# Hashed attention and SwiGLU on one Trainium2 core: key signs of the early pairs moved from VectorE to ScalarE, query signs spread by a transfer

## The chip, the cores and the metric

The kernel runs on one core of one Trainium2 chip. The metric is the device time of one execution in microseconds (us); smaller is better. The times are those of whole executions without the profiler; the profile is one further execution, recorded by the hardware profiler, whose span is a little different from the timed median.

## What is computed

Two blocks follow each other. The first is attention in which a key counts for a query only if both fall in the same hash bucket; the second is a SwiGLU feed-forward block on its output.

```python
q_bits = (einsum('bhsd,dk->bhsk', q, proj) > 0)      # 6 bits; k_bits likewise
mask   = q_bucket[..., :, None] == k_bucket[..., None, :]
scores = where(mask, (q @ k.T) / sqrt(64), -1e9)
attn   = exp(scores - max) ; attn /= sum(attn) + 1e-9
x      = (attn @ v)   # (4, 8, 768, 64) -> (3072, 512)
out    = (silu(x @ w_gate) * (x @ w_val)) @ w_out     # d_ff 1536
```

There are 4 batches of 8 heads, 768 positions and head size 64; everything is float32 (the weights come as 64-bit floats and are narrowed on the chip).

## The kernel before

**Units of work.** Two heads make a *pair* (`n` = 0 to 15, four to a batch), because two heads of size 64 fill 128 partitions. A pair is worked in two *halves* of 384 queries, and each half in six *chunks* `c` of 128 keys. For each chunk `score` (L461) makes a score tile for either head on TensorE: first the product of the transposed float32 queries and keys (`qT`, `kT`), then a second bf16 matmul into the same PSUM tile with the *sign tiles* `qb`, `kb`. ScalarE takes the exponential (L464) into the weight tile `A` (or its early place, called `room`). VectorE adds the weight tiles of the six chunks (`add`, L489 and L493) into `acc`. After the six chunks come six chunks of `attend` (L475): weights times values into one PSUM bank `av`, which ScalarE copies out (L482).

**The mask by signs.** `hash_w` projects the 64 numbers of a head to 6; either head has a group of 16 rows in a block of 32. `Sign` on ScalarE (L397) turns the projected queries and keys into +1 and -1 in rows 0 to 31 of `qb`, `kb`. A seventh row of the group is a constant. VectorE then spreads these rows to where the matmul of either head reads them (rows 0 to 63 for head 0, rows 64 to 127 for head 1): the keys' rows are multiplied, once for head 0 and once for head 1, by a column that is OFF/2 = 2^34 for this head's bits, -6 times that for its constant row and 0 for the other head (L406, two instructions), and the queries' rows are copied (L409, one instruction). The second matmul so adds 0 where all six bits agree and -2^35 or less where they don't.

**Sum and normalisation.** For pair n-1, `total` is issued in the first half of pair n, behind the second chunk's scores: a matmul with ones sums `acc` over the partitions (L506, into the `av` bank, for batch 0), VectorE takes the reciprocal (L514), eight transfers on the SyncE queue spread it over the partitions (L519), and `norm` on VectorE multiplies (L526). In batch 0 the `av` bank is free for the next `attend` only when the reciprocal has read it.

**Order of the work.** The order is written out by hand, and each engine works through its own list in order. In the first batch (pairs 0 to 3), there is no feed-forward work yet for TensorE; VectorE and ScalarE fill up with narrowing the weights (L279, L280, L293, L295, L298, L327). From pair 4 on, TensorE's list is filled up with the feed-forward matmuls of the batch before (L550). The next pair's operands are made one pair ahead (`front(n + 1)`): for pairs 1 to 4 by TensorE transposes (L378) that ScalarE copies out (L381), and by `hash_at_once`, which projects (L391) and takes the four signs behind the last chunk of the second half; its spread waits in the list `rest` until the end of that half, so that VectorE reaches it behind the six `add`s. For pairs 5 to 15, `hash_blocks` hands signs and spread to the feed-forward stretch one by one, and the queries' signs are spread by a SyncE transfer (L411). PSUM has seven rotating banks and the `av` bank. `load(n + 2)` puts the loads of queries, keys and values on the SyncE queue behind the second half's `attend`.

Two lines of the main loop say where the preparation is issued:

```python
if u + c == 2 or not gating and half == 1 and c == NCH - 1:
    prepare_pair(1)
```

Of the kernel before, what the change touches and what calls it, by code (L numbers as in the profile page):

```python
# [8 lines left out]
FP32 = mybir.dt.float32  # L9
# [3 lines left out]
ALU = mybir.AluOpType  # L13
AF = mybir.ActivationFunctionType
AX = mybir.AxisListType
# [3 lines left out]
def kernel(  # L19
# [31 lines left out]
    OFF = 2.0**35  # L51
    SCALE = 1.0 / D**0.5
# [4 lines left out]
    konst = ctx.enter_context(tc.tile_pool(name="konst", bufs=1))  # L57
# [12 lines left out]
    def bank(name):  # L70
        return banks.tile([P, 512], FP32, tag="ps", name=name)
# [50 lines left out]
    ident = konst.tile([P, P], FP32, tag="ident", name="ident")  # L122
# [9 lines left out]
    for _ in range(9):  # L132
        ps = bank("idle")
# [4 lines left out]


    HR = 16  # L140
    assert NBITS + 1 <= HR and 2 * HR == BLOCK
    rules = wraw.tile([P, PIECE, 2], I32, tag="words", name="rules").rearrange("p f w -> p (f w)")
    rules = rules.bitcast(FP32)[:, 0 : 3 * P].rearrange("p (x r) -> p x r", r=P)

    nc.gpsimd.memset(rules[:, 0, :], -(2.0**-120))
    nc.gpsimd.memset(rules[:, 1:3, :], 0.0)
    groups = rules.rearrange("p x (g r) -> p x g r", r=HR)
    nc.gpsimd.memset(groups[:, 0, :, NBITS : NBITS + 1], 1.0)
    for h in range(2):
        g = groups[:, 1 + h, h, :]  # L150
        nc.gpsimd.memset(g[:, 0:NBITS], OFF / 2)
        nc.gpsimd.memset(g[:, NBITS : NBITS + 1], -NBITS * OFF / 2)
    nc.vector.tensor_tensor(rules, rules, ident.unsqueeze(1).to_broadcast([P, 3, P]), op=ALU.mult)
    columns = konst.tile([P, 3], FP32, tag="columns", name="columns")
    nc.vector.tensor_reduce(out=columns, in_=rules, axis=AX.X, op=ALU.add)
    nudge, *times_k = (columns[0:BLOCK, x : x + 1] for x in range(3))

    hash_w = konst.tile([P, BLOCK], FP32, tag="hash", name="hash")
    nc.vector.memset(hash_w, 0.0)
# [14 lines left out]
    for t in (sides["k", 0], sides["q", 0], sides["q", 1]):  # L174
# [19 lines left out]
                      name="room")  # L194
# [160 lines left out]
    def prepare_on(n):  # L355
        for _ in range(n):
            next(preparing, None)
# [7 lines left out]
    T = {}  # L365
    bits = {}
# [3 lines left out]
    def front(n):  # L370


        def transpose(name, half):
            if (name, n) not in T:
                T[name, n] = opnd.tile([P, S], FP32, tag=name + "T", name=name + "T")
            ps = bank("tps")
            for i in range(CH):
                nc.tensor.transpose(ps[:, i * P : (i + 1) * P],  # L378
                                    raws[name, n][:, half * CH + i, :, :].rearrange("p h d -> p (h d)"),
                                    ident)  # L380
            nc.scalar.copy(T[name, n][:, half * HQ : (half + 1) * HQ], ps[:, 0:HQ])  # L381

        bits["q", n] = sides["q", n % 2]
        bits["k", n] = sides["k", n % 2]

        def hash_blocks(todo, own):


            tile_ = bank("hps")
            for i, (name, half) in enumerate(todo):  # L390
                nc.tensor.matmul(tile_[i * BLOCK : (i + 1) * BLOCK, 0:HQ], hash_w,  # L391
                                 T[name, n][:, half * HQ : (half + 1) * HQ],
                                 start=True, stop=True)
            low, high = slice(0, BLOCK), slice(D, D + BLOCK)

            def sign(i, name, half):
                nc.scalar.activation(bits[name, n][low, half * HQ : (half + 1) * HQ],  # L397
                                     tile_[i * BLOCK : (i + 1) * BLOCK, 0:HQ], AF.Sign, bias=nudge)

            def spread():  # L400
                for name in sorted({name for name, _ in todo}):
                    hs = [half for x, half in todo if x == name]
                    b = bits[name, n][:, hs[0] * HQ : (hs[-1] + 1) * HQ]
                    if name == "k":
                        for to, times in ((high, times_k[1]), (low, times_k[0])):
                            nc.vector.tensor_scalar(b[to], b[low], scalar1=times, scalar2=None,  # L406
                                                    op0=ALU.mult)
                    elif own:
                        nc.vector.tensor_copy(b[high], b[low])  # L409
                    else:  # L410
                        nc.sync.dma_start(b[high], b[low])  # L411

            return [lambda i=i, at=at: sign(i, *at) for i, at in enumerate(todo)] + [spread]

        def hash_at_once(todo):
            *signs, spread = hash_blocks(todo, True)
            for f in signs:
                f()
            return [spread]

        def transpose_blocks(name):
            T[name, n] = opnd.tile([P, S], FP32, tag=name + "T", name=name + "T")
            nc.vector.transpose(T[name, n], raws[name, n].rearrange("p c h d -> p (c h d)"))

        order = [("q", 0), ("q", 1), ("k", 0), ("k", 1)]
        if n > NP:

            return ([lambda name=name: transpose_blocks(name) for name in "qk"]
                    + [lambda: hash_blocks(order, False)])
        turns = [lambda x=x: transpose(*x) for x in order]  # L430
        if n == 0:
            return [turns[2], turns[0], lambda: hash_at_once([("k", 0)]),
                    lambda: hash_at_once([("q", 0)]), turns[3], turns[1],
                    lambda: hash_at_once([("k", 1), ("q", 1)])]
        return turns[2:] + turns[:2] + [lambda: hash_at_once(order)]


    units = [(n, half, c) for n in range(len(pairs)) for half in range(2) for c in range(NCH)]
# [9 lines left out]
    def weights(u):  # L448
        return ((early_ring if u < MOVE else late_ring) + ring)[u % NCH]

    def score(u):
        n, half, c = units[u]
        qs = slice(half * HQ, (half + 1) * HQ)
        ks = slice(c * P, (c + 1) * P)
        sc = [bank("sc")[:, 0:HQ] for _ in range(2)]
        for x, start in ((T, True), (bits, False)):
            if u < 2 and not start:
                prepare_pair(1)
            for h in range(2):
                rows = slice(h * D, (h + 1) * D)  # L460
                nc.tensor.matmul(sc[h], x["k", n][rows, ks], x["q", n][rows, qs],  # L461
                                 start=start, stop=not start)
        for h in range(2):
            nc.scalar.activation(weights(u)[:, h, 0:HQ], sc[h], AF.Exp, scale=SCALE)  # L464

    def attend(u):
        n, half, c = units[u]
# [16 lines left out]
    def add(u):  # L484
        n, half, c = units[u]
        a = weights(u)
        if c == 1:
            acc[n, half] = att.tile([P, 2, HQ], FP32, tag="acc", name="acc")
            nc.vector.scalar_tensor_tensor(out=acc[n, half], in0=weights(u - 1)[:, :, 0:HQ],  # L489
                                           scalar=S * EPS / P, in1=a[:, :, 0:HQ],  # L490
                                           op0=ALU.add, op1=ALU.add)
        elif c > 1:
            nc.vector.tensor_tensor(acc[n, half], acc[n, half], a[:, :, 0:HQ], op=ALU.add)  # L493
# [241 lines left out]
    for u in range(0, N, NCH):  # L735
        n, half, _ = units[u]
        gating = u >= LATE
# [3 lines left out]
                nc.gpsimd.memset(t[:, :, HQ:AW], 1.0)  # L741
        for c in range(NCH):
            score(u + c)
            if u + c == 2 or not gating and half == 1 and c == NCH - 1:
                prepare_pair(1)
                if u == 0:
                    finish(rest)
            if c == 1 and half == 0 and 0 < n <= NP:
                total(n - 1)
            if c:  # L750
                add(u + c)
        if n <= NP:
            finish(waiting)
        if not gating and half == 0:
            steps = front(n + 1)
        if not gating and half == 0 and u > 0:
# [9 lines left out]
        if not gating and half == 0:  # L766
            prepare_pair(2 if u > 0 else 4)
        finish(first)
        finish(rest)
        prepare_on(0 if u == LATE else 4)  # L770
        chores = []
        if half == 1 and n >= NP:
# [67 lines left out]
```

The softmax here doesn't subtract the row's maximum and nothing guards it: scores larger than these inputs give would overflow.

## Time and profile before

| what | before |
|---|---|
| time, median of 3 (lowest to highest) | 1007.15 us (1006.15 to 1009.98) |
| span of the profiled execution | 1005.8 us |
| TensorE busy in 0 to 120, 120 to 920, 920 to the end | 109.52 of 120, 799.4 of 800, 82.5 of 86 us |
| VectorE busy in 30:40, 50:60, 80:90, 100:110 | 9.53, 9.35, 9.57, 9.35 of 10 us |
| ScalarE busy in the same stretches | 9.29, 6.53, 6.86, 5.89 of 10 us |
| share of the 16 DMA engines in them | 0.64, 0.77, 0.98, 1.00 |

How to read it: a line of a timeline gives the start, the time from the first start to the last end of a run of like instructions, the engine, the line of the kernel, the operation with `out<-in`, and in square brackets how long the engine sat idle before it and what ended that wait. In the table of groups, the number after "x" is the count, then busy us and the mean ns of one, then the idle time before. In the list of waits, the columns are total us, number of times and longest. The chain of waits goes back from the last instruction to whatever released each step, so it shows which engine held the others up in which stretch. TensorE's matmul ends are modelled, and its "busy" includes matmuls that run longer at a lower granted clock.

### The profile page before, as it was taken

To read this page: it belongs to the slowest core of one execution; us is meant where nothing else is said; L and a number is where in the kernel's file an instruction comes from. 1 tells how busy PE (TensorE), PEld (TensorE's weight loads), DVE (VectorE), ACT (ScalarE), POOL (GpSimd) and SP (SyncE) were. 2 spreads that over 40 slices of the span, in tenths; PEclk is the share of its full clock that TensorE was granted. 3 is DMA by queue.
4 is the path that set the end of the run, shared out by engine and by line. 5 is a ranking of instruction groups with operands and counts; after the bars stand their busy time and mean duration, and the time that the engine had idled before them with its cause. 6 is when DMAs were issued, how large, how long until landed. Compare 5 with 4: busy or idle time off the path is not lost.

```text
span 1005.8 us, 12454 instructions
## 1 busy us (share of the span) xinstructions
PE 991.4 (99%) x4597; PEld 600.8 (60%) x4597; DVE 577.2 (57%) x904; ACT 392.3 (39%) x877; POOL 101.0 (10%) x195
## 2 busy tenths in 40 slices
PE   9988899999999999999999999999999999999998
PEld 4444455555566775555557776555555787555687
DVE  5888898888884615556454543545556442435431
ACT  6877456555433214334341223334443211222200
POOL 3222132231000000000000000000000000111000
PEclk9999999999999999999999999999999999999999
DMA  7776586876313032423430304242122011323001
GB/s 228 215 243 215 157 214 186 230 241 180 103 37 84 24 76 83 105 91 90 105 107 23 75 20 116 76 104 83 56 85 80 22 37 63 104 77 115 29 28 36
DMA packets 120557, 106.75 MB, mean 106 GB/s; under 512 B 89200, under 2 KB 103888, under 8 KB 120496
## 3 DMA queue, kind: packets, MB, share of 16 engines
q0 software_dynamic: 19104, 73.28, 22.8%
q1 hardware_dynamic: 100592, 32.48, 14.1%
q8 instruction: 36, 0.59, 0.2%
q10 hardware_dynamic: 800, 0.20, 0.1%
q14 instruction: 25, 0.20, 0.1%
HBM read 81.79 MB, written 17.30 MB: 99 GB/s over the span
## 4 chain that ended last, share of the span: by engine, by line
PE 89%; DVE 6%; DMA 1%; SPq 1%; issue 1%; ACT 1%; DVEq 0%; POOL 0%
PE up L550 43%; PE po L550 21%; PE sc L461 12%; PE av L475 10%; DVE acc L493 1%; SPq L519 1%; PE sum L506 1%; PE hps L391 1%; DMA words<-in_moe_w_out_dram 1%; DVE wo L514 1%; DVE room L295 1%; DVE room L327 1%; DMA wo<-wo 1%; DVE room L293 0%; PE idle L134 0%
## 5 line engine op out<-in xcount | busy, mean ns | idle before, releaser
L550 PE MATMUL up<-xT,room 128*128 128x384 f32 x768 | 260.9, 488 | 0.0
L550 PEld LDWEIGHTS up<-xT,room 128*128 128x128 f32 x768 | 144.6, 190 | 106.7 <-issue 9.8
L550 PE MATMUL up<-xc,room 128*128 128x384 f32 x576 | 197.4, 486 | 0.0
L461 PE MATMUL sc<-qT,kT 64*128 64x384 f32 x768 | 162.3, 498 | 0.5 <-DVE c L537 0.5
L550 PEld LDWEIGHTS up<-xc,room 128*128 128x128 f32 x576 | 109.4, 190 | 76.3
L493 DVE TENSOR_TENSOR acc<-acc,A 128x768 f32<-128x768 f32 x128 | 122.7, 958 | 15.4 <-ACT A L464 1.8
L309 POOL DMA_DIRECT2D room<-ram x96 | 51.9, 541 | 714.7 <-PE up L550 707.6
L554 DVE TENSOR_TENSOR c<-c,up 128x384 f32<-128x384 f32 x72 | 39.9, 554 | 138.3 <-PE up L550 137.9
L464 ACT ACTIVATE A<-sc 128x384 f32<-128x384 f32 x256 | 105.4, 504 | 7.5 <-PE sc L461 7.5
L461 PEld LDWEIGHTS sc<-qT,kT 64*128 64x128 f32 x768 | 68.7, 189 | 53.8 <-issue 46.8
L685 ACT COPY o<-po 128x256 f32<-128x256 f32 x48 | 17.9, 372 | 200.5 <-PE po L550 200.5
L475 PE MATMUL av<-A,vraw 128*64 128x384 f32 (+1 forms) x512 | 88.2, 486 | 0.0
L536 ACT ACTIVATE th<-c 128x384 f32<-128x384 f32 x72 | 37.6, 523 | 127.5 <-DVE c L537 88.8
L461 PE MATMUL sc<-qb,kb 64*128 64x384 bf16 x384 | 66.2, 325 | 8.4 <-DVE kb L406 8.4
L554 DVE TENSOR_TENSOR o<-o,po 128x256 f32<-128x256 f32 x36 | 15.2, 421 | 99.0 <-PE po L550 70.0
L464 ACT ACTIVATE room<-sc 128x384 f32<-128x384 f32 x128 | 54.2, 496 | 40.8 <-PE sc L461 40.8
L550 PE MATMUL po<-wo,hid 128*128 128x256 f32 x288 | 66.9, 382 | 0.0
L550 PE MATMUL po<-wo,room 128*128 128x256 f32 x288 | 66.3, 379 | 0.1
L550 PE MATMUL po<-room,hid 128*128 128x256 f32 x288 | 66.1, 379 | 0.0
L475 PEld LDWEIGHTS av<-A,vraw 128*64 128x64 f32 x512 | 36.7, 137 | 46.1 <-issue 45.2
L613 ACT COPY c<-up 128x384 f32<-128x384 f32 x72 | 34.4, 478 | 69.7 <-PE up L550 69.7
L550 PEld LDWEIGHTS po<-wo,hid 128*128 128x128 f32 x288 | 54.1, 190 | 12.1 <-issue 4.9
(107 smaller groups left out, 967.8 us busy)
## 6 DMA issues: line engine op xcount, KB each, us to landing
room<-ram POOLq DMA_DIRECT2D x48, 512.0 KB, 4.7
room<-ram POOLq DMA_DIRECT2D x48, 384.0 KB, 3.9
vraw<-in_v_dram SPq DMA_DIRECT2D x16, 384.0 KB, 3.2
ram<-room POOLq DMA_DIRECT2D x12, 512.0 KB, 5.0
out_dram<-o SPq DMA_DIRECT2D x48, 128.0 KB, 1.7
room<-in_moe_w_out_dram POOLq DMA_DIRECT2D x10, 512.0 KB, 6.3
qraw<-in_q_dram SPq DMA_DIRECT2D x48, 96.0 KB, 3.2
hid<-in_moe_w_gate_dram POOLq DMA_DIRECT2D x9, 512.0 KB, 6.8
```

Source lines behind the costliest of these rows:

```text
L295: nc.vector.scalar_tensor_tensor(out=wi, in0=hi, scalar=-(1 << 31), in1=wi, op0=ALU.bitwise_and, op1=ALU.bitwise_or)
L309: nc.gpsimd.dma_start(places[k % 2][:, PARTS[go], :], ram[k % NG][:, PARTS[go], :])
L327: nc.vector.tensor_tensor(o, x, y, op=op)
L461: nc.tensor.matmul(sc[h], x["k", n][rows, ks], x["q", n][rows, qs], start=start, stop=not start)
L464: nc.scalar.activation(weights(u)[:, h, 0:HQ], sc[h], AF.Exp, scale=SCALE)
L475: nc.tensor.matmul(ps[h * D : (h + 1) * D, 0:width], raws["v", n][:, h, c, :], a[:, h, 0:width], start=c == 0, stop=c == NCH - 1)
L493: nc.vector.tensor_tensor(acc[n, half], acc[n, half], a[:, :, 0:HQ], op=ALU.add)
L536: nc.scalar.activation(th, g, AF.Tanh, scale=0.5)
L550: nc.tensor.matmul(ps, a, x, start=start and i == 0, stop=i == len(pairs_) - 1, skip_group_check=True)
L554: nc.vector.tensor_tensor(o, a, b, op=op)
L613: nc.scalar.copy(tile_of(g, spot), c)
L685: nc.scalar.copy(o, c)
```

## The change

It touches pairs 1 to 4 above all, whose signs VectorE spreads in the middle of its work of the first batch.

- **Key signs by ScalarE for either head.** `Sign` now takes a scale and a bias column per head. For head h the scale column (`mask[h]`) is 1 in this head's rows and 0 in the others', and the bias column (`one_head[h]`) is a tiny negative number in the bit rows and -1 in six constant rows. The result is written directly where that head's matmul reads it. There are four such instructions (two halves, two heads) in place of two, and no multiplication on VectorE.
- **A power of two.** The signs are no longer multiplied by 2^34. Instead the keys of pairs 0 to 4 are scaled by 2^-34 as they are copied out of the transpose, and the exponential's scale is 2^34 times as large. All early scores are so scaled alike. Six constant rows of -1 (queries' side +1) replace one row of -6.
- **Query signs by a transfer.** The queries' signs of pairs 1 to 4 are spread by a SyncE transfer that stands in front of the loads of pair n+2 in that queue; to have it there, the hash is issued one chunk earlier (behind chunk 4), and the queries' two signs stand ahead of the last chunk's exponentials. The keys' four signs stand behind these.
- **Pair 0** keeps VectorE for its spread; **pairs 5 to 15** keep the two multiplications, but the transfer and the multiplications are two entries of the feed-forward stretch now, where they were one.
- The columns are made from a 32 x 8 x 32 tile, not from 128 x 3 x 128.

```diff
-    nudge, *times_k = (columns[0:BLOCK, x : x + 1] for x in range(3))
+    nudge = {"q": columns[0], "k": columns[1]}
+    one_head = columns[2:4]
+    mask, times_k = columns[4:6], columns[6:8]
...
-            nc.scalar.copy(T[name, n][:, half * HQ : (half + 1) * HQ], ps[:, 0:HQ])
+            nc.scalar.activation(T[name, n][:, half * HQ : (half + 1) * HQ], ps[:, 0:HQ], AF.Copy,
+                                 scale=2 / OFF if name == "k" else 1.0)
...
-                    if name == "k":
-                        for to, times in ((high, times_k[1]), (low, times_k[0])):
-                            nc.vector.tensor_scalar(b[to], b[low], scalar1=times, scalar2=None,
-                                                    op0=ALU.mult)
-                    elif own:
-                        nc.vector.tensor_copy(b[high], b[low])
-                    else:
-                        nc.sync.dma_start(b[high], b[low])
-            return [lambda i=i, at=at: sign(i, *at) for i, at in enumerate(todo)] + [spread]
...
+        def hash_early(todo):
+            q0, q1, *ks = hash_blocks(todo)
+            q0()
+            q1()
+            spread_q()
+            return [lambda k=k, h=h: k(to=(low, high)[h], bias=one_head[h], scale=mask[h])
+                    for k in ks for h in range(2)]
+
+        def hash_late(todo):
+            return hash_blocks(todo) + [spread_q, lambda: spread_k(times_k)]
...
-        return turns[2:] + turns[:2] + [lambda: hash_at_once(order)]
+        return turns[2:] + turns[:2] + [lambda: hash_early(order)]
...
-            nc.scalar.activation(weights(u)[:, h, 0:HQ], sc[h], AF.Exp, scale=SCALE)
+            nc.scalar.activation(weights(u)[:, h, 0:HQ], sc[h], AF.Exp,
+                                 scale=SCALE * (OFF / 2 if n <= NP else 1.0))
...
-            if u + c == 2 or not gating and half == 1 and c == NCH - 1:
+            if u + c == 2 or not gating and half == 1 and c == NCH - 2:
                 prepare_pair(1)
-                if u == 0:
-                    finish(rest)
...
         if n <= NP:
             finish(waiting)
+            finish(rest)
...
         finish(first)
-        finish(rest)
```

More of the change, by code (lines that the diff above doesn't have):

```diff
@@ L140 @@
     HR = 16
-    assert NBITS + 1 <= HR and 2 * HR == BLOCK
+    assert 2 * NBITS <= HR and 2 * HR == BLOCK
     rules = wraw.tile([P, PIECE, 2], I32, tag="words", name="rules").rearrange("p f w -> p (f w)")
-    rules = rules.bitcast(FP32)[:, 0 : 3 * P].rearrange("p (x r) -> p x r", r=P)
-    nc.gpsimd.memset(rules[:, 0, :], -(2.0**-120))
-    nc.gpsimd.memset(rules[:, 1:3, :], 0.0)
+    rules = rules.bitcast(FP32)[0:BLOCK, 0 : 8 * BLOCK].rearrange("p (x r) -> p x r", r=BLOCK)
+    NUDGE = -(2.0**-120)
+    nc.gpsimd.memset(rules[:, 2:8, :], 0.0)
+    nc.gpsimd.memset(rules[:, 0:2, :], NUDGE)
     groups = rules.rearrange("p x (g r) -> p x g r", r=HR)
-    nc.gpsimd.memset(groups[:, 0, :, NBITS : NBITS + 1], 1.0)
+    nc.gpsimd.memset(groups[:, 0, :, NBITS : 2 * NBITS], 1.0)
+    nc.gpsimd.memset(groups[:, 1, :, NBITS : 2 * NBITS], -1.0)
     for h in range(2):
[L150 to L155, printed above, removed]
-    nudge, *times_k = (columns[0:BLOCK, x : x + 1] for x in range(3))
+        nc.gpsimd.memset(groups[:, 2 + h, h, 0:NBITS], NUDGE)
+        nc.gpsimd.memset(groups[:, 2 + h, h, NBITS : 2 * NBITS], -1.0)
+        nc.gpsimd.memset(groups[:, 4 + h, h, 0 : 2 * NBITS], 1.0)
+        nc.gpsimd.memset(groups[:, 6 + h, h, 0 : 2 * NBITS], OFF / 2)
+    nc.vector.tensor_tensor(rules, rules,
+                            ident[0:BLOCK, 0:BLOCK].unsqueeze(1).to_broadcast([BLOCK, 8, BLOCK]),
+                            op=ALU.mult)
+    columns = konst.tile([P, 8], FP32, tag="columns", name="columns")
+    nc.vector.tensor_reduce(out=columns[0:BLOCK], in_=rules, axis=AX.X, op=ALU.add)
+    columns = [columns[0:BLOCK, x : x + 1] for x in range(8)]
+    nudge = {"q": columns[0], "k": columns[1]}
+    one_head = columns[2:4]
+    mask, times_k = columns[4:6], columns[6:8]
     hash_w = konst.tile([P, BLOCK], FP32, tag="hash", name="hash")
@@ L380, in transpose, with hash_blocks @@
                                     ident)
-            nc.scalar.copy(T[name, n][:, half * HQ : (half + 1) * HQ], ps[:, 0:HQ])
+            nc.scalar.activation(T[name, n][:, half * HQ : (half + 1) * HQ], ps[:, 0:HQ], AF.Copy,
+                                 scale=2 / OFF if name == "k" else 1.0)
         bits["q", n] = sides["q", n % 2]
         bits["k", n] = sides["k", n % 2]
-        def hash_blocks(todo, own):
+        low, high = slice(0, BLOCK), slice(D, D + BLOCK)
+        def hash_blocks(todo):
             tile_ = bank("hps")
@@ L393, in hash_blocks @@
                                  start=True, stop=True)
[L394 to L403, printed above, removed]
-                    if name == "k":
-                        for to, times in ((high, times_k[1]), (low, times_k[0])):
-                            nc.vector.tensor_scalar(b[to], b[low], scalar1=times, scalar2=None,
-                                                    op0=ALU.mult)
-                    elif own:
-                        nc.vector.tensor_copy(b[high], b[low])
-                    else:
-                        nc.sync.dma_start(b[high], b[low])
@@ L413, in hash_blocks, with sign @@
-            return [lambda i=i, at=at: sign(i, *at) for i, at in enumerate(todo)] + [spread]
-        def hash_at_once(todo):
-            *signs, spread = hash_blocks(todo, True)
-            for f in signs:
-                f()
-            return [spread]
+            def sign(i, name, half, to=low, **how):
+                nc.scalar.activation(bits[name, n][to, half * HQ : (half + 1) * HQ],
+                                     tile_[i * BLOCK : (i + 1) * BLOCK, 0:HQ], AF.Sign,
+                                     **(how or {"bias": nudge[name]}))
@@ new lines, in hash_blocks, with spread_k, spread_q, hash_own @@
+            return [lambda i=i, at=at, **how: sign(i, *at, **how) for i, at in enumerate(todo)]
+        def spread_k(times, cols=slice(0, S)):
+            b = bits["k", n][:, cols]
+            for to, by in ((high, times[1]), (low, times[0])):
+                nc.vector.tensor_scalar(b[to], b[low], scalar1=by, scalar2=None, op0=ALU.mult)
+        def spread_q():
+            nc.sync.dma_start(bits["q", n][high], bits["q", n][low])
+        def hash_own(*todo):
+            for f in hash_blocks(todo):
+                f()
+            for name, half in todo:
+                cols = slice(half * HQ, (half + 1) * HQ)
+                if name == "k":
+                    spread_k(mask, cols)
+                else:
+                    nc.vector.tensor_copy(bits["q", n][high, cols], bits["q", n][low, cols])
@@ L428, in front @@
             return ([lambda name=name: transpose_blocks(name) for name in "qk"]
-                    + [lambda: hash_blocks(order, False)])
+                    + [lambda: hash_late(order)])
         turns = [lambda x=x: transpose(*x) for x in order]
         if n == 0:
-            return [turns[2], turns[0], lambda: hash_at_once([("k", 0)]),
-                    lambda: hash_at_once([("q", 0)]), turns[3], turns[1],
-                    lambda: hash_at_once([("k", 1), ("q", 1)])]
-        return turns[2:] + turns[:2] + [lambda: hash_at_once(order)]
+            return [turns[2], turns[0], lambda: hash_own(("k", 0)), lambda: hash_own(("q", 0)),
+                    turns[3], turns[1], lambda: hash_own(("k", 1), ("q", 1))]
+        return turns[2:] + turns[:2] + [lambda: hash_early(order)]
     units = [(n, half, c) for n in range(len(pairs)) for half in range(2) for c in range(NCH)]
```

## The prediction

> **What bounds the kernel now.** I read the page first. TensorE is busy 99% of the span, so the question is where the missing time and the slow matmuls lie.
>
> ```profile
> PE 991.4 (99%) x4597; PEld 600.8 (60%) x4597; DVE 577.2 (57%) x904; ACT 392.3 (39%) x877; POOL 101.0 (10%) x195
> ```
>
> The list of waits, for TensorE in the first 120 us, names what it loses there; from 120 us on it shows one wait of 0.5 us.
>
> ```profile
> PE sc L461 <- DVE kb L406: 8.4, 4, 2.7
> PE av L475 <- DVE wo L514: 0.7, 2, 0.4
> ```
>
> Next the timeline of TensorE at one such place (pair 2's first half; like waits of 2.49 and 2.75 us end at 83.11 and 108.26).
>
> ```profile
> 53.48 0.92 PE L461 MATMUL sc<-qT,kT 64*128 64x384 f32 x4
> 57.04 0.61 PE L461 MATMUL sc<-qb,kb 64*128 64x384 bf16 x2 [2.64 <-DVE kb L406]
> ...
> 58.39 1.51 PE L506 MATMUL sum<-acc,ones 128*32 128x384 f32 x8
> ```
>
> The scores wait for the spread keys' signs, and then the sum takes 1.51 us, against 0.85 in the unstalled pair 1. Unstalled, this half (36 score matmuls 5.05, sum 0.78, transposes 0.80 in the chain) is 6.63 us. It took 11.53 (53.48 to 65.01), 10.20 less 0.36 for the reciprocal in pair 3, and 10.82 against 5.83 (no transposes) in pair 4: 4.9 + 3.2 + 5.0 = 13.1 us are lost, 7.9 of them waiting. Why the signs are late the timeline of VectorE shows.
>
> ```profile
> 51.86 4.15 DVE L493 TENSOR_TENSOR acc<-acc,A 128x768 f32<-128x768 f32 x4
> 56.04 0.85 DVE L406 TENSOR_SCALAR kb<-kb,columns 32x768 bf16<-32x768 bf16 x2
> 56.93 0.35 DVE L409 COPY qb<-qb 32x768 bf16<-32x768 bf16 x1
> ...
> 61.60 2.55 DVE L514 RECIPROCAL wo<-sum 128x384 f32<-128x384 f32 x1
> ...
> 71.38 1.02 DVE L526 SCALAR_TENSOR_TENSOR xT<-xT,e,wo 128x768 f32<-128x768 f32 x1 [2.16 <-DMA wo<-wo]
> ```
>
> VectorE runs back to back from add to spread to weights to reciprocal, then waits for the spread reciprocal. The chain of waits agrees: from 30.36 to 108.26 it has no TensorE piece, only VectorE, the SyncE queue and transfers, and from 108.26 TensorE all but alone. So the first batch is bound by the loop **adds, spread, weights, reciprocal (L514), eight transfers (L519), norm (L526), adds**; TensorE only follows.
>
> **What the Trainium skill says.** "ScalarE: Activation LUTs" (What ACT_TABLE_LOAD costs) gives each pointer operand of an ACTIVATE about 93 ns. The trace agrees in direction: the 384-wide exponential takes 504 ns, Sign with a bias column 575. "TensorE: Matmul & The Clock Gate" (What's actually happening) says that an idle window of about 3.4 us, at a phase that is not fixed, drops the clock to half. The trace agrees roughly: after 2.64 and 2.75 us of waiting, sums took 1.51 us, after 2.49 us 0.85. "DMA: Bandwidth & Descriptors" (Issuing engines are not separate DMA queues) says all queues share the same 16 DMA engines; here a qb transfer lands 1.9 us after issue in the median, and 6.7 at worst.
>
> ```profile
> L397 ACT ACTIVATE kb<-hps,columns 32x384 bf16<-32x384 f32 x32 | 18.4, 575 | 1.2 <-PE hps L391 0.6
> ```
>
> **The change, part by part.** *VectorE.* For pairs 1 to 4, two multiplications and a copy go: 56.04 to 57.29 is 1.25 us each time, all on the loop, 5.0 us in sum.
>
> *ScalarE.* Two more signs per pair, and the keys' four have two columns. Price of one: at least 575 ns (the row), at most 575 + 93 = 668 (the skill). Starts in the trace are 585 ns apart, so with the upper value, which I take, 4 x 0.675 = 2.70 us against 2 x 0.54 = 1.08 from the first key sign to the next operation (29.01 to 30.09): ScalarE is 1.6 us later (1.1 at the lower price). Queued behind are the weight scaling (L279, L280), the copy L482 and the next exponentials. Pair 1 is the tight place, since ScalarE is busy without a gap from 20.3 to 33: the scaling of the next piece ends at 30.76 + 1.55 = 32.3, and VectorE, 1.25 us earlier, would want it at 32.96 - 1.25 = 31.7. So 0.6 us of the first 1.25 is lost, which leaves 0.65. The copy L482 then ends near 33.35, just when the sum wants its bank (33.33). For pairs 2 to 4 VectorE is far behind ScalarE's scaling (piece scaled at 43.4, used at 57.9), so nothing is lost.
>
> *Will the signs be there?* In pair 2 the exponentials of chunk 4 end at about 48.6 (49.72 less two of 0.37 and 0.38 for an earlier start), query signs to 49.8, chunk 5 to 50.5, key signs to 53.2. Scores start at 53.1 and want the signs at 53.9: 0.7 us in hand, and only the first half's columns are needed first. The transfer issues at 49.8 and lands at 51.7 (median); head 1 wants it at 54.0. In hand 2.3 us, and about 2 in pairs 1, 3, 4.
>
> *Loads.* They stood on SyncE at 21.76 (pair 2) and 44.27 (pair 3); now they wait for the query signs, to about 28.9 and 50.3. Keys of pair 2 then issue by 31.6 and, at 3.8 us in the median, land at 35.4, in front of their transposes at 37.54. Later ones have over 8 us. So nothing.
>
> *The new waits.* With signs no longer late, TensorE meets the loop at two other places: the sum (L506) needs the last add, and `attend` needs the bank that the reciprocal reads. Step by step, from the trace's times less what VectorE has saved:
> - Pair 1: reciprocal ends at 38.74 - 0.65 = 38.1; attend starts at 38.4, not 38.79.
> - Pair 2: last add 56.0 - 0.65 = 55.4, TensorE at the sum at 54.95: wait 0.5. Reciprocal ends 64.15 - 0.65 - 1.25 = 62.25; TensorE, at 60.35, waits 1.9.
> - Pair 3: last add 82.05 - 1.9 = 80.15, TensorE at 78.85: wait 1.3. Reciprocal ends 89.9 - 3.15 = 86.75; wait 1.65.
> - Pair 4: last add 107.2 - 3.15 = 104.05; TensorE at 103.3: wait 0.75. The reciprocal began 0.17 late behind its sum, so it ends at 113.7 - 0.17 - 4.4 = 109.15; wait 1.0. Attend starts at 109.2, not 115.42: **6.2 us earlier** (4.55 of the loop and 1.7 by which TensorE lagged behind the reciprocal because of its stall and slow clock).
> - Feed-forward starts 4.05 later, at 113.25 (before 119.53). Norm is bound to the reciprocal by transfers: 120.72 - 113.7 = 7.0, so it ends at 109.15 + 7.0 + 1.0 = 117.15. The third group of up matmuls reads pair 3, its second half 3.25 us after the start, at 116.5: wait 0.65.
> Sum: 6.2 - 0.65 = 5.6 us. No wait is over 1.9 us, so I take no slow clock; a slow stretch would lie in front of a wait anyway and shorten it.
>
> *From 118 us on* TensorE is its own bound (799.4 of 800 us busy from 120 to 920), and everything moves along. VectorE lags 1 us more there, but waits for TensorE from 131 on. The separated entries of pairs 5 to 15 let one VectorE operation past the multiplications, which nobody on TensorE waits for. The head (columns of 32 rows) is hidden by the loads in front of the first transposes at 5.14. Copies and exponentials with another constant cost the same.
>
> **Rivals.**
> - *ScalarE and transfers give part back.* For: ScalarE has only some 0.5 us spare in pair 1 and 0.1 us in front of the sum of pair 2, and DMA is 0.6 to 1.0 busy. If 1.5 us later exponentials reach the loop in two pairs, 3 us go: 1004.5. Against: VectorE's adds come 1 us and more behind the exponentials.
> - *More comes back.* With the loads gone from behind the spread reciprocal's transfers (44.27 follows 44.17 at once), norm may start earlier by the 1.5 to 2.2 us it waits, for two or three pairs: some 3 us, 998.5. Against: with DMA busy, the 1.9 us of landing is no queueing.
> - *Slower.* Every qb transfer lands at the worst 6.7 us, and keys of pair 2 at their worst 8.5: TensorE waits 2.6 + 2.6 + 2.5 + 2.1 + 2.2 = 12 us, against the 8.4 + 0.7 removed, with a like slow clock: 1007.15 + 3 = 1010. For: DMA is full in 80:90 and 100:110. Against: the 32 like transfers of L519 landed in 2.0 us in the median in just this stretch.
>
> **How the numbers follow.** The forecast case, 1007.15 - 5.6 = 1001.5 us, 0.62; part given back 0.20; more 0.12; slower 0.06. With the lower price of a sign, pair 1 saves 0.5 more (1001.0); with the loop's 0.6 us lost in another pair, 1002. The range 998.5 to 1004.5 takes in the first case, most of the third and half of the second. Half a per cent is 5.0 us, so faster holds most of the forecast case and all of the third, 0.66; same 0.28; slower 0.06.
>
> **What would show it.** The wait of L461 on L406 gone; waits of L506 on the adds (0.5 to 1.3 us) and of L475 on L514 (1 to 1.9) in its place; attend of pair 4 at 109 and the up matmuls at 113; sums of 0.85 us; key signs of 575 to 670 ns. Wrong would be: scores waiting for ScalarE's kb or the qb transfer, transposes at 37.5 waiting for keys, VectorE idle before L293 or the adds in later pairs, or norm more than 7 us behind the reciprocal.

## The result and the profile after

| | before | after |
|---|---|---|
| time, median (lowest to highest) | 1007.14 us (1006.15 to 1009.98) | 1014.5 us (1013.16 to 1015.26) |
| span of the profiled execution | 1005.8 us | 1011.0 us |
| feed-forward (`up` matmuls) begins | 119.53 us | 124.78 us |
| from there to the end of the span | 886.3 us | 886.2 us |

The ratio is 1.0067, 95% interval 1.0044 to 1.009: slower, where 1001.5 us had been forecast. All of the 5.2 us between the two spans lie ahead of the feed-forward, in the same first 120 us or so that the prediction is about. (The profiled execution after is the fastest of its four, 1013.16 us, so the spans lie closer together than the medians, which differ by 7.4 us.) (Lines have moved: the key signs are L407, the spread on VectorE L416, the transfer L419, scores L484, `attend` L499, sum L530, reciprocal L538, its transfers L543, norm L550, `up` L574, the transposes of keys L386.)

The busy line of the page shows that the two engines moved as planned: VectorE has 6 us less, ScalarE 7 us more.

```profile
PE 994.2 (98%) x4597; PEld 601.7 (60%) x4597; DVE 571.1 (56%) x892; ACT 399.0 (39%) x885; POOL 101.6 (10%) x200
```

The list of waits of TensorE in the first 120 us (total, times, longest) shows what took the place of the 8.4 us:

```profile
PE tps L386 <- DMA kraw<-in_k_dram: 4.8, 1, 4.8
PE tps L386 <- issue: 4.7, 1, 4.7
PE sc L484 <- DMA qb<-qb: 1.4, 1, 1.4
...
PE sc L484 <- DVE kb L416: 0.5, 1, 0.5
```

The wait for VectorE's spread is gone but for 0.5 us in pair 0. In its place TensorE stands twice for 4.7 us in front of the *transposes* of the next pair's keys. The timeline of TensorE at the first of them, in pair 2's first half (start, length, engine, line, operation, in brackets the idle time):

```profile
55.31 1.79 PE L530 MATMUL sum<-acc,ones 128*32 128x384 f32 x8
...
60.20 0.33 PE L484 MATMUL sc<-qb,kb 64*128 64x384 bf16 x2
65.25 1.51 PE L386 MATMUL tps<-ident,kraw 128*128 128x128 f32 x6 [4.72 <-issue]
66.69 2.84 PE L499 MATMUL av<-room,vraw 128*64 128x386 f32 x8
69.32 3.53 PE L499 MATMUL av<-A,vraw 128*64 128x386 f32 x16
```

Before, the same three groups, unstalled, took 0.87, 1.52 and 2.76 us:

```profile
64.21 0.87 PE L378 MATMUL tps<-ident,kraw 128*128 128x128 f32 x6
65.01 1.52 PE L475 MATMUL av<-room,vraw 128*64 128x386 f32 x8
66.36 2.76 PE L475 MATMUL av<-A,vraw 128*64 128x386 f32 x16
```

So 4.7 us of waiting brought 2.7 us more of slow matmuls. The granted clock was 0.50 there and 1.00 before the wait. In a line of a 2 us stretch it is the third figure from the end, in front of the DMA share and the GB/s:

```profile
66.00:68.00 2.00, 2.00 (x8) 0.89 (x8) 1.90 (x2) 1.70 (x4) 0.00 (x0) 0.50 1.03 385
```

At the second place (96.20, wait 4.75) it was 2.6 us again. The sum at 55.31 is another matter: it took 1.79 us at a granted clock of 1.00, since its weight loads waited for VectorE's last add, which the prediction had expected (at 0.5 us):

```profile
56.25 0.15 PEld L530 LDWEIGHTS sum<-acc,ones 128*32 128x32 f32 x6 [0.81 <-DVE acc L517]
```

Waits and slow stretches come to 4.72 + 4.75 + 1.40 + 2.7 + 2.6 = 16.2 us, and with 0.9 us for that sum to 17.1. The late signs had cost 13.1 us by the prediction's count, and 12.5 if each half is set against what pair 1's first half took unstalled (6.03 us from 31.51 to its transposes at 37.54; the prediction has 5.83); two waits for the reciprocal had cost another 0.7. That accounts for 3.9 of the 5.2 us; the rest I did not follow.

"issue" in the list means that the records name no releaser. The SyncE queue's timeline does (start, time to issue):

```profile
49.81 0.51 SPq L419 DMA_DIRECT2D qb<-qb  x1
50.42 1.30 SPq L94 DMA_DIRECT2D qraw<-in_q_dram  x2
51.77 1.33 SPq L94 DMA_DIRECT2D kraw<-in_k_dram  x2
53.51 0.95 SPq L81 DMA_DIRECT2D vraw<-in_v_dram  x1
62.98 6.16 SPq L543 DMA_DIRECT2D wo<-wo  x8
80.11 0.51 SPq L419 DMA_DIRECT2D qb<-qb  x1
...
82.08 9.13 SPq L94 DMA_DIRECT2D kraw<-in_k_dram  x2
```

and that of the kernel before, at the first of these places:

```profile
44.27 1.29 SPq L94 DMA_DIRECT2D qraw<-in_q_dram  x2
45.61 1.34 SPq L94 DMA_DIRECT2D kraw<-in_k_dram  x2
```

Loads that went out at 44.3 to 46.9 now stand behind the query signs' transfer, which waits for ScalarE, and go out at 50.4 to 53.1. The second of the two key loads, issued at 52.46, landed 12.7 us later, at 65.16, and at 65.25 the transposes began. Six us late would still do, with the landing time of before (3.6 to 5.5 us for keys in 40:110). But the keys now land in 6.9 to 13.3 us, 10.0 in the median (counted from the start of their issue; the 13.3 us contain an issue of 7.08). The transfers' packets in stretches of 2 us say why; the figures after the queue's name are packets, MB, and share of the time of 16 engines. After, at 52:54, 54:56 and 60:62 (q1 is the SyncE queue, q0 that of GpSimd):

```profile
q1 hardware_dynamic: 1359, 0.34, 75.1%
...
q0 software_dynamic: 118, 0.44, 69.5%
q1 hardware_dynamic: 314, 0.08, 17.4%
...
q0 software_dynamic: 188, 0.69, 86.0%
q1 hardware_dynamic: 191, 0.08, 14.3%
```

Queries and keys of a pair are 4 x 768 = 3072 packets of 256 bytes. Some 1500 of them pass until 54; then GpSimd's own transfers start, its weight loads and its traffic with DRAM (`ram`), and SyncE's queue falls to between 175 and 655 packets in 2 us until 64. The Trainium skill, "DMA: Bandwidth & Descriptors" (Queues, rings and completion order), says that each DMA engine goes round between the queues that have work, one packet at a time. If that holds for the packets of these records, small packets must give way to large ones; this is an inference. The trace agrees at 60:62 (188 large packets against 191 small ones), but not at 56:58, where it was 78 against 655.

In pair 4's turn it is worse by one step, which the chain of waits shows (start, length, what):

```profile
53.51 15.10 DMA vraw<-in_v_dram
68.62 3.09 DMA wo<-wo
...
82.08 7.08 SPq L94
89.20 6.86 DMA kraw<-in_k_dram
96.20 1.51 PE tps L386 x6
97.71 5.98 PE av L499 x24
```

The values' load, issued with the others, lands only at 68.61, and the last of the reciprocal's eight transfers goes out at that moment, as the SyncE queue's list of waits has it:

```profile
SPq L543 <- DMA vraw<-in_v_dram: 1.0, 1, 1.0
```

That transfer then took 3.1 us, so norm came at 71.80, 8.9 us behind the reciprocal's end and not 7.0. And of pair 4's two key loads the first took 7.08 us merely to be issued, so the second went out only at 89.20, 2.3 us before TensorE wanted it (91.45). The chain of the first batch, which before ran through VectorE and had no TensorE piece between 30 and 108 us, now runs from 53.51 on for the most part through these loads and the TensorE work behind them.

### The profile page after: what moved, and what is told of

Its sections match the earlier page's. It is cut to its first block, busy times and chain, and to the rows that moved or that the text cites. A ratio compares the mean times of both kernels' runs of the same rounds, so it can differ in the third digit from the quotient of the medians.

```text
span 1011.0 us, 12464 instructions
## 1 busy us (share of the span) xinstructions
PE 994.2 (98%) x4597; PEld 601.7 (60%) x4597; DVE 571.1 (56%) x892; ACT 399.0 (39%) x885; POOL 101.6 (10%) x200
## 4 chain that ended last, share of the span: by engine, by line
PE 92%; DMA 3%; ACT 2%; DVE 1%; SPq 1%; issue 1%; POOL 0%; DVEq 0%; ACTq 0%
PE up L574 42%; PE po L574 21%; PE sc L484 13%; PE av L499 11%; DMA vraw<-in_v_dram 1%; PE sum L530 1%; PE hps L402 1%; SPq L94 1%; ACT A L487 1%; DMA words<-in_moe_w_out_dram 1%; PE tps L386 1%; DMA kraw<-in_k_dram 1%; PE idle L134 0%; DVE room L358 0%; ACT kb L407 0%
## 5 line engine op out<-in xcount | busy, mean ns | idle before, releaser
L574 PE MATMUL up<-xT,room 128*128 128x384 f32 x768 | 261.1, 488 | 0.0
L574 PEld LDWEIGHTS up<-xT,room 128*128 128x128 f32 x768 | 144.5, 190 | 106.9 <-issue 9.8
L574 PE MATMUL up<-xc,room 128*128 128x384 f32 x576 | 197.4, 486 | 0.0
L484 PE MATMUL sc<-qT,kT 64*128 64x384 f32 x768 | 161.0, 494 | 0.4 <-DVE c L561 0.4
L574 PEld LDWEIGHTS up<-xc,room 128*128 128x128 f32 x576 | 109.4, 190 | 76.3 <-ACT hid L637 0.2
L484 PEld LDWEIGHTS sc<-qT,kT 64*128 64x128 f32 x768 | 67.7, 186 | 55.5 <-issue 46.1
L499 PE MATMUL av<-A,vraw 128*64 128x384 f32 (+1 forms) x512 | 89.6, 492 | 0.0
L484 PE MATMUL sc<-qb,kb 64*128 64x384 bf16 x384 | 65.5, 323 | 1.9 <-DMA qb<-qb 1.4
L574 PE MATMUL po<-wo,hid 128*128 128x256 f32 x288 | 66.9, 382 | 0.0
L574 PE MATMUL po<-wo,room 128*128 128x256 f32 x288 | 66.3, 379 | 0.1
L574 PE MATMUL po<-room,hid 128*128 128x256 f32 x288 | 66.1, 379 | 0.0
L499 PEld LDWEIGHTS av<-A,vraw 128*64 128x64 f32 x512 | 37.4, 139 | 47.9 <-issue 46.0
L574 PEld LDWEIGHTS po<-wo,hid 128*128 128x128 f32 x288 | 54.1, 190 | 12.1 <-issue 4.9
```

Source lines behind the costliest of these rows:

```text
L499: nc.tensor.matmul(ps[h * D : (h + 1) * D, 0:width], raws["v", n][:, h, c, :], a[:, h, 0:width], start=c == 0, stop=c == NCH - 1)
L574: nc.tensor.matmul(ps, a, x, start=start and i == 0, stop=i == len(pairs_) - 1, skip_group_check=True)
```

## The experiments

Two theories for the loss. **A:** the loads of pair n+2 stand behind the query signs' transfer in the SyncE queue, go out 6 us late, and land in the midst of GpSimd's traffic; TensorE waits for them and slows. **B:** what was moved is itself the cost: ScalarE's longer signs, the earlier hash, the extra transfers. The first four ran together (before: 1007.43 us median).

### Loads first

The change with the loads of queries and keys ahead of the second half's scores, so ahead of the transfer.

```diff
+        ahead = not gating and half == 1 and n + 2 < len(pairs)
+        if ahead:
+            for name in "qk":
+                fetch(n + 2, name, nc.sync)
         for c in range(NCH):
             score(u + c)
...
-            load(n + 2)
+            if ahead:
+                fetch(n + 2, "v", nc.sync)
+            else:
+                load(n + 2)
```

> The changed kernel, with the loads of queries and keys of pair n+2 put on the SyncE queue ahead of the second half's scores, so in front of the query signs' transfer; the values' load stays. Theory A (the loads of pairs 3 and 4, held behind the transfer, land in the busy stretch of the weight loads, and TensorE's transposes wait 4.7 us each): these two waits and the slow clock behind them go, the loop of the first batch shows what it saved, 1000.5 to 1004 us. Rival B (two more and dearer signs on ScalarE and the added traffic cost what VectorE saves, the held loads are only where it shows): TensorE waits elsewhere, 1006 us or more.

**1002.54 us, ratio 0.9958 (0.9946 to 0.997).** Theory A. TensorE's waits in the first 120 us:

```profile
PE av L499 <- DVE wo L538: 3.2, 3, 1.7
...
PE sc L484 <- DVE kb L416: 0.5, 1, 0.5
PE sc L484 <- DMA qb<-qb: 0.3, 1, 0.3
...
PE sum L530 <- DVE acc L517: 0.2, 1, 0.2
```

These are the waits that the prediction had named, for the reciprocal and for the last add, and no others of weight. Where `attend` begins in pairs 2, 3 and 4:

```profile
63.06 1.52 PE L499 MATMUL av<-room,vraw 128*64 128x386 f32 x8 [1.67 <-DVE wo L538]
...
87.11 1.52 PE L499 MATMUL av<-room,vraw 128*64 128x386 f32 x8 [1.30 <-DVE wo L538]
...
109.02 1.52 PE L499 MATMUL av<-room,vraw 128*64 128x386 f32 x8 [0.27 <-DVE wo L538]
```

The same loads, at 46:48 and 48:50 of this kernel's trace, have the DMA engines nearly to themselves:

```profile
q1 hardware_dynamic: 1923, 0.48, 111.1%
...
q1 hardware_dynamic: 1129, 0.28, 85.1%
q0 software_dynamic: 30, 0.12, 15.1%
```

3052 packets in 4 us. ScalarE's signs, the earlier hash and the transfers are all in this kernel: B falls as the cause of the loss.

### The transfer alone

The kernel before, with VectorE's copy of the query signs replaced by a SyncE transfer ahead of the loads (pairs 1 to 4); the key signs stay with VectorE.

```diff
                     elif own and n > 0:
+                        pass
...
+            if n > 0:
+                nc.sync.dma_start(bits["q", n][D : D + BLOCK], bits["q", n][0:BLOCK])
```

> The kernel before with one part of the change alone: the queries' signs of pairs 1 to 4 are spread by a SyncE transfer, issued behind the signs and so in front of the loads of pair n+2, in place of VectorE's copy (L409). Theory A: the transposes of pairs 3 and 4 wait for keys here too, though VectorE has 0.35 us less per pair to do: pair 3 at 64.2 waits 1 us or less, since TensorE comes there 4 us later than in the changed kernel, pair 4 waits 4 to 7 us; slower than before by 3 to 9 us. Rival B: no slower, 1005.5 to 1007.5 us.

**1013.73 us, ratio 1.0064 (1.0046 to 1.0082).** Put into the old kernel alone, the transfer loses nearly as much as the whole change (6.3 us by the medians, against 7.4), within the 3 to 9 expected. One place is as expected in kind; its line in TensorE's timeline (of the slowest of six executions, 1017.3 us):

```profile
68.90 1.51 PE L378 MATMUL tps<-ident,kraw 128*128 128x128 f32 x6 [5.35 <-DMA kraw<-in_k_dram]
```

But it stands in pair 3's transposes, where I expected at most 1 us; pair 4's keys were in time, and at two later places the scores waited for the query signs' transfer instead (5.8 us together, the longest 3.7). So in this one trace and in the one of the changed kernel TensorE meets different late transfers; both kernels have the same transfer in front of the loads.

### VectorE's copy instead of the transfer

The changed kernel, with the query signs of pairs 1 to 4 copied by VectorE as before, and so nothing ahead of the loads.

```diff
-            spread_q()
-            return [lambda k=k, h=h: ...
+            copy = lambda: nc.vector.tensor_copy(bits["q", n][high], bits["q", n][low])
+            return [copy] + [lambda k=k, h=h: ...
```

> The changed kernel with the queries' signs of pairs 1 to 4 copied by VectorE as before (one copy of 0.35 us per pair), so that nothing holds the loads; ScalarE's six signs stay. Theory A: loads as before, VectorE saves 0.85 us per pair, 3.4 us on the loop: 1002 to 1005 us. Rival B: 1007 us or more, with TensorE waiting for signs or ScalarE.

**1004.88 us, ratio 0.9972 (0.9964 to 0.998).** So the key signs on ScalarE, with the earlier hash, bring 2.5 us (3.4 expected), and the transfer, with the loads out of its way, another 2.3. Between this kernel and the changed one, 9.6 us slower, lies nothing but the transfer in place of the copy. The copy keeps part of the old wait, as the list shows:

```profile
PE sc L484 <- DVE qb L438: 4.4, 3, 1.9
```

### Keys first

The change with the order keys, queries, values in `load`, so that the keys go out 1.4 us earlier.

```diff
-        for name in "qkv":
+        for name in "kqv":
```

> The changed kernel with the keys' load ahead of the queries' in every load; still behind the transfer. The transposes of the keys come some 10 us ahead of those of the queries, so the keys are what is waited for. Theory A: keys are issued 1.3 us earlier, and in pair 4 ahead of the slow issue at 82 to 91: the waits of 4.7 us fall to 1 to 3.5 us, and 1006 to 1012 us. Rival B: within 1 us of the changed kernel, 1014.

**1007.26 us, ratio 1.0013 (0.9997 to 1.0028).** The keys now take 4.8 us in the median to land (3.2 to 10.1), and TensorE waits for them nowhere, where 1 to 3.5 us were expected: 1.4 us at the right moment are worth 7 of the 12 us between after and loads first, by the medians (3 of the 14 executions took 1011.85 to 1013.91 us). The queries behind them take 8.5 us (4.9 to 12.7) and have more time in hand. The rest shows behind the SyncE queue: norm waits 3.64 us for the reciprocal's transfers in pair 3's first half, and 3.58 in pair 4's. Behind the one the adds are late and TensorE's sum waits for them, behind the other the first feed-forward matmuls wait for norm's result:

```profile
PE av L499 <- DVE wo L538: 3.6, 3, 1.7
PE sum L530 <- DVE acc L517: 3.0, 3, 1.6
PE up L574 <- DVE xT L550: 2.1, 1, 2.1
```

### Thinner weight loads

Is being late enough, or does it need the collision? The change with its loads left where they are, but each GpSimd load of weight words from the eleventh piece on carries a quarter of its bytes; part of the weights is left out, and the feed-forward multiplies other numbers. (The cleared tiles make the start 1.6 us later, to be taken off.)

```diff
+    for t in middle[2:]:
+        nc.gpsimd.memset(t, 0)
...
+                if i >= 10:
+                    nc.gpsimd.memset(words[i], 0)
+            w = PIECE // 2 if i >= 10 else 2 * PIECE
-            queue.dma_start(words[i].rearrange("p f w -> p (f w)"), pieces[i][1])
+            queue.dma_start(words[i].rearrange("p f w -> p (f w)")[:, 0:w], pieces[i][1][:, 0:w])
```

> The changed kernel with the loads left where it puts them (behind the query signs' transfer), but every GpSimd load of weight words from the eleventh piece on moves a quarter of its bytes (128 KB for 512 KB), so part of the weights is left out and the feed-forward works on other numbers; the instructions are the same. It separates being late from colliding. Theory A (the loads are only hurt because they meet the 2 MB of weight loads issued at 53.35): the keys of pair 3 issue near 52 as before, but land in 4 to 6 us in place of 10; TensorE's transposes at 60.5 and 91 wait less than 0.5 us, the weights times values behind them run at 1.5 us per eight, and the time is 1000.5 to 1004 us. Rival C (six us late is enough, whatever else the DMA engines carry: the SyncE queue itself or the 256-byte packets make the loads slow): landing stays above 8 us, the transposes still wait 3 us or more, and the time is 1011 to 1015.

**1005.83 us, ratio 0.9978 (0.9965 to 0.9991)**, or about 1004.2 without the later start: of the 12 us some 10 are back, though the time is just above A's range. Not all of that is the keys' doing. In the profiled execution the feed-forward begins at 119.97, or 118.4 without the later start, against 124.78 after and 113.12 in loads first; another 1.7 us come from behind that point (884.5 us to the end, 886.2 after), where these transfers are thinner too.

The two pairs part. In pair 4 the thinner queue cleared the way: the wait for keys is 0.36 us and not 4.75. The packets of 86:88, first after and then here, show it:

```profile
q0 software_dynamic: 173, 0.64, 79.2%
q1 hardware_dynamic: 574, 0.14, 32.0%
...
q1 hardware_dynamic: 1335, 0.34, 76.8%
q0 software_dynamic: 93, 0.25, 36.8%
```

So there the collision is shown. In pair 3 the expectation missed, and both of C's signs came: the keys still landed in 10.1 us in the median, and TensorE waited more than 3 us:

```profile
65.59 1.51 PE L392 MATMUL tps<-ident,kraw 128*128 128x128 f32 x6 [3.24 <-DMA kraw<-in_k_dram]
```

The DMA view of 56:58 gives a likely reason:

```profile
q0 software_dynamic: 108, 0.41, 74.5%
q1 hardware_dynamic: 328, 0.08, 18.3%
```

GpSimd's queue is as full there as before. Three transfers with DRAM of 1.4 MB in all, issued at 53.64 to 55.26 ahead of the weight loads, were not thinned; they took 7.1 to 9.0 us to land, and from 54 to 62 GpSimd's queue moved 1.55 MB in all. So A was probably too narrow when it named the weight loads: the keys meet all that GpSimd moves. For pair 3 this is argued and not shown, since no run thins the transfers with DRAM. Against C speaks the kernel before, where the values' load at 53.62 has the SyncE queue to itself and still takes 10.0 us to land in this stretch, and 3.2 at 31.65. TensorE also waited 2.8 us here for two query-sign transfers, which A had not named.

### Two versions of loads first

These two ran with the former one (before: 1007.81). In the first, the hash goes back behind the last chunk; in the second, pair 0's second half scales its next weight piece on ScalarE ahead of the key signs.

```diff
-            if u + c == 2 or not gating and half == 1 and c == NCH - 2:
+            if u + c == 2 or not gating and half == 1 and c == NCH - 1:
```

> The kernel with the loads of queries and keys ahead of the second half's scores, and with the hash back behind the last chunk (behind chunk 5, as in the kernel before) in place of chunk 4. It asks whether the earlier hash is needed once the loads don't queue behind the transfer. Theory: ScalarE has the same work in front of the key signs, only the query signs and their transfer come about 1 us later, with some 2 us in hand, so 1001.5 to 1004 us and no wait of the scores over 0.5 us. Rival: the transfer, later by 1 us and in the same crowd of weight loads, is awaited by the scores 0.5 to 1.5 us in two or three pairs: 1004 to 1008.

```diff
             finish(waiting)
+            if n == 0 and half == 1:
+                scale_ahead()
             finish(rest)
...
-        for _ in range(1 if u else 2):
+        for _ in range(2 if u == 0 else 0 if n == 0 and half == 1 else 1):
             scale_ahead()
```

> The kernel with the loads of queries and keys ahead of the second half's scores, and in pair 0's second half the scaling of the next weight piece on ScalarE stands in front of the four key signs, not behind them. In pair 1 VectorE waits 0.99 us for that scaling in the loop of adds, weights, reciprocal and norm. Theory: this wait goes, the reciprocal of pair 1 and all of the loop is 1.0 us earlier, the key signs end 1.3 us later but their first half still before 32.15, when the scores want them: 1001 to 1002 us (1.0 less than the 1002.5 of the loads first alone). Rival: the signs are then late for pair 1's first scores (a wait of 0.5 to 1.5 us there), or the gain is lost at a later wait of TensorE: 1002.5 to 1004.

The late hash gave **1002.1 us (0.9932 to 0.9964)**, the same as loads first: with the loads out of the way, the earlier hash isn't needed. One wait of 0.9 us for the query signs appeared, where none over 0.5 was expected, but the last reciprocal started at 105.86, no later than the 106.41 of loads first. The scaling ahead gave **1000.88 us (0.993, 0.9917 to 0.9943)**, just under the 1001 to 1002 expected: VectorE's 0.99 us of waiting for L287 in pair 1 is gone, and the last reciprocal starts at 105.33 and not at 106.41. This is the fastest version of the study, 0.7% under the kernel before and, by the medians, 1.3% under the changed one.

## Why the prediction was wrong

**The step that failed is "Loads".** It said of the loads held by the transfer: keys of pair 2 "land at 35.4, in front of their transposes at 37.54. Later ones have over 8 us. So nothing." For pair 2 this held: no wait at 37.74. For pairs 3 and 4 the term was not nothing: TensorE waited 4.72 and 4.75 us for their keys and then ran 2.7 and 2.6 us longer at the slow clock. In pair 3 the time in hand was what I said, 8.1 to 8.8 us (issue at 51.77 and 52.46, transposes wanted at 60.53), but I set against it the 3.8 us median of the kernel before, and the keys took 7.2 and 12.7 us. In pair 4 the first load had 9.4 us and took 13.3, 7.08 of them to be issued; the second, held behind it, had 2.3 us left and took 6.9. The trace of before could have told: there the values' load that went out in this very stretch, at 53.62, took 10.0 us to land. I used the worst landing of before, 8.5 us, for pair 2 only, in a rival at 6% with the query signs' transfer as its main cost. A load that is moved has the landing time of the place to which it moves.

**What rested on it.** "No wait is over 1.9 us, so I take no slow clock" fell with it: the 4.7 us waits halved TensorE's speed for some 6 us each (the granted clock is 0.50 in 66:70). The Trainium skill's idle window of about 3.4 us in "TensorE: Matmul & The Clock Gate" (What's actually happening), cited in the prediction, agrees with these waits. The seven us from reciprocal to norm fell too: 8.9 us in pair 2's first half, since the last of the eight transfers went out only when the values' load had landed and was slow itself. (In pair 1's first half they were 7.8 us in the changed kernel and in loads first alike, so that excess is not the held loads'.) I had named "transposes at 37.5 waiting for keys" and "norm more than 7 us behind the reciprocal" among the signs of being wrong; the second came, the first a pair later.

**What held, by loads first, which takes away only the failed step.**

| step | predicted | loads first |
|---|---|---|
| sum held up by the last add, pairs 2, 3, 4 | 0.5, 1.3, 0.75 us | 1.0, 0.8, 0 us |
| pair 2: reciprocal free, attend starts | 62.25, wait 1.9 | 63.06, wait 1.67 |
| pair 3: attend starts | 86.75, wait 1.65 | 87.11, wait 1.30 |
| pair 4: attend starts | 109.2, wait 1.0 | 109.02, wait 0.27 |
| feed-forward starts | 113.25 | 113.12 |
| norm in pair 4's first half begins | 116.1 | 115.37 |
| `up` waits for norm | 0.65 us | none |
| time | 1001.5 us | 1002.54 us |

(The sums are read from their start to the next scores, 1.82, 1.62 and 0.78 us, less the 0.78 of an unstalled one; the list of waits shows only 0.2 us, because part of a sum's wait falls on its weight loads.) The start of the feed-forward came out to within 0.2 us; from the feed-forward's start to the end it was 887.3 us, 1.0 more than before. That is the microsecond by which the time exceeds 1001.5; it was not followed.

VectorE's part was right in sum: the last reciprocal of the first batch starts at 106.41 in loads first and at 111.19 before, 4.8 us earlier, and 4.55 had been reckoned. The steps to it fit less well. Pair 2's reciprocal starts at 60.40 in the changed kernel and at 61.60 before, 1.2 us earlier and not 1.9, because norm in pair 1's first half came 0.8 us late; shorter ways from reciprocal to norm in pairs 3 and 4 (6.5 and 6.4 us in loads first, and not 7.0) made up for part of it. That the sum fits so well is in part luck. The four key signs took 2.76 us from the first start to the next operation (predicted 2.70), so the skill's price for a pointer operand, which I took, was right: the early two-column signs last up to 672 ns, the others 577 in the median. In pair 1 VectorE waited 0.99 us for ScalarE's scaling, where 0.6 us was to be lost, but it came there earlier than reckoned, so the reciprocal ended at 38.13 as forecast (38.1); the last version shows that the wait was real and could be had back. Query signs by transfer were in time in loads first but for 0.3 us; in the changed kernel 1.4 us was lost to them.

**The rivals.** None had the cause. "Slower" had its kind, late transfers and a slow clock, but took the query signs' transfer for the main one, and was priced at 1010. That transfer cost 1.4 us in the changed kernel, though 5.8 in the transfer alone.

**Open:** whether GpSimd's transfers with DRAM are what held pair 3's keys, and why one issue of the key loads took 7.08 us at 82.08 in the changed kernel, with no wait in the records. Other loads behind the transfer show the like (7.69 us for the queries at 104.42 in keys first, to issue four loads), but no run separates the cause.

## What to carry to other kernels

The SyncE queue took its transfers in the order of the program: one that waits for ScalarE, put in front of loads, held them for 6 us here, and with the loads in front of it the kernel is 12 us faster. So put a transfer that waits for a compute engine behind loads that could go at once. Before a load is moved in time, look up what the DMA engines carry at its new place, and take its landing time from there, not from a median over the kernel. When a stall of TensorE is taken away, check which longer wait could come in its place; here one of 4.7 us cost another 2.7 us at the slow clock.

## What was not expected of the hardware

- The keys of pairs 3 and 4, in packets of 256 bytes, landed in 3.7 to 4.3 us where GpSimd's queue was nearly empty (loads first) and in 6.9 to 13.3 us where it was busy (after; the 13.3 with 7.08 of issue). Their bytes (0.8 MB for queries and keys) are fewer than the 2.9 MB that GpSimd moved from 52 to 64. SyncE's queue fell from 1923 packets in 2 us to as few as 175.
- Cutting the weight loads to a quarter did not speed up the keys of pair 3 (10.1 us in the median, 10.0 before the cut): GpSimd's transfers with DRAM, not thinned, are the likely reason. In pair 4, where the weight loads were the larger part of what the queue was given, the same cut let SyncE's queue send 1335 packets in 2 us in place of 574.
- The order of two equal loads in a queue, 1.4 us apart, was worth 7 us.
